# Where the weight sums of the seven-product form are made: eight sets in feed-forward steps 22 to 54, instead of four beside the weight decode and four in steps 22 to 36

## The chip, the cores and the metric

The kernel runs on one core of a Trainium2 chip. The metric is the device time of one execution in microseconds; lower is better. Engines are named as in the profile: PE (TensorE, the matrix unit), DVE (VectorE), ACT (ScalarE), POOL (GpSimd), SP (SyncE, which here only issues DMAs).

## The reference, cut to what matters

Eight batches of eight heads of sliding-window attention with a linear bias, then one feed-forward layer over the 4608 tokens, all in float32.

```python
scores = q @ k.T / sqrt(64)                 # q, k, v: (8, 8, 576, 64)
scores = where(0 <= rel < 128, scores - slope[h] * abs(rel), -1e9)
attn = softmax(scores) @ v
x = attn.transpose(0, 2, 1, 3).reshape(4608, 512)
h = x @ w_in                                # (512, 2048)
out = (h * sigmoid(1.702 * h)) @ w_out      # (2048, 512)
```

## The kernel before, in words

**Precision.** A float32 operand of the feed-forward layer is cut into a rounded high part and the rest (`res[:, 0]`, `res[:, 1]`; `xh`, `xl`; `gh`, `gl`), and a product of two operands is three matrix products: high by high, and the two mixed ones. ACT makes the high part with a cast, POOL makes the rest with a subtraction.

**Weights.** `w_in` and `w_out` are cut into 16 slices each, `w1[f]` and `w2[f]`, of 128x512 elements. They arrive as 64-bit words and are turned into split float32 by `decode`: an ACT operation into a tile `wc` (L226), two DVE operations by way of a PSUM tile `bits` (L228, L229), an ACT cast (L232) and a POOL subtraction (L233) into `w`. `bits` is taken from the PSUM ring `h_ps`, which has two buffers and also holds the up-projections. `wc` is taken from the SBUF ring with the tag `o`, which has five buffers (`OBUFS`) and also holds `wr`, `wh`, `xb`, `half` and `o`.

**Feed-forward, first form.** Tokens come in 18 chunks of 256. Chunks 0 to 11 are computed directly. One step is one slice `f` of one chunk: `up` (L579, 12 matrix products 128x256 into `h_ps`), the activation (ACT L584, DVE L585 into `g`, ACT L588 `gh`, POOL L589 `gl`), and `down` (L599, 6 products 128x512 into `acc0` and `acc1`). There are 192 such steps: chunk 0 with its first 8 slices (steps 0 to 7), chunk 1 (8 to 23), chunk 0's other 8 slices (24 to 31), then chunks 2 to 11. Between the two parts of chunk 0 its partial sums go to DRAM: ACT copies `acc` into `half` (L616), which frees `acc`, and SP writes it out (L618); at step 31 DVE adds it again (L623, L624).

**Decode.** Slices are decoded just ahead of the step that needs them, so decoding lasts until slice 15 of chunk 1, step 23.

**Attention.** One `tick` moves the attention units one stage further: loads (SP, L166), splits of q, k and v (ACT, and POOL L318, L329, L330), scores (PE L342 or L352), bias and minimum (DVE L369 or L380), exponents (ACT L392 or L399), normalisation (ACT L417 and POOL L420, or DVE L424), transposes (PE L438 or L461), and the product with v (PE L495 or L518). Batches 0 and 1 use one form, the lines named first; batches 2 to 7 use the second, heavier on DVE and POOL, and pass through `xb` (ACT L548) and DVE additions (L554, L557). Ticks are paced so that a chunk's tokens are there in time.

**Feed-forward, second form.** Chunks 12 to 17 are computed in pairs, with seven products instead of eight for each pair of weight slices (2j, 2j+1). This needs sums of weight blocks, S1 to S4, split again. `sums(j, a, b)` makes them: four DVE operations 128x256 in place (L653 to L656), then for each of the two tiles an ACT cast into `wh` (L659), a POOL subtraction (L660), and four DMAs of 128 KB (L663, L664) into DRAM tiles `part`. That is one set; there are eight, j = 0 to 7. `copy_out` writes the plain blocks (L641). The pairs read the parts from DRAM through a ring, after step 191.

**When the sums are made.** For j = 4 to 7 `decode_next` calls `sums` at once after it has decoded slice 2j+1, on the two tiles `wc` that the decode has just used: `kept` holds the first of them until the second is there. For j = 0 to 3 the `wc` tiles are long gone, so `rebuilt` adds the two parts of the split weight again (L646, DVE 128x512, into `wr`), two such additions a set, in steps 22, 25, 29 and 32:

```python
if made < F0 // 2 and now >= REBUILT[len(REBUILT) * made // (F0 // 2)]:
    sums(made, rebuilt(2 * made), rebuilt(2 * made + 1))
```

**What sets the order.** The program is written in this order, and a scheduler then places each instruction on its engine by its own estimate of times, under the data dependencies and the rings' buffers; each engine runs its own list strictly in order, and SP's list holds nearly all DMAs. So a change in one place moves instructions on all engines for a long way.

Of the kernel before, what the change touches and what calls it, by code (L numbers as in the profile page):

```python
# [24 lines left out]
NF = DFF // P  # L25
# [16 lines left out]
F0 = 8  # L42
# [5 lines left out]
COLS = 2 * P  # L48
RING = 5
LEAD = 6  # L50
REBUILT = range(22, 36)
COPIED = 64
COVER = 2
ORDER = "A11", "A12", "S2", "S3", "S1", "S4", "A22"
# [98 lines left out]
def tile_kernel(ctx: ExitStack, tc: tile.TileContext, q0, k0, v0, qT, kT, v, w_in, w_out, out):  # L153
# [51 lines left out]
    w1, w2 = [None] * NF, [None] * NF  # L205
# [7 lines left out]
        w1[f] = fetch(w_in[f], f"w1_{f}")  # L213
        w2[f] = fetch(w_out[f], f"w2_{f}")

    kept = {}

    def decode(st, name, pin=lambda ins: ins):

        words = st.bitcast(I32).rearrange("p (m two) -> p m two", two=2)  # L220
        top, low = words[..., 1], words[..., 0]
        c = ffn.tile([P, 512], I32, name="wc", tag="o", bufs=OBUFS)

        pin(nc.scalar.activation(c.bitcast(F32), top.bitcast(F32), AF.Prelu, scale=2.0 ** -112, alpha=2.0 ** 32))  # L226
        bits = ps.tile([P, 512], I32, name="bits", tag="h_ps", bufs=2)
        pin(nc.vector.tensor_scalar(bits, low, 29, None, ALU.logical_shift_right))  # L228
        pin(nc.vector.scalar_tensor_tensor(c, c, 3, bits, ALU.logical_shift_left, ALU.bitwise_or))  # L229
        w = c.bitcast(F32)  # L230
        res = const.tile([P, 2, 512], F32R, name=name, tag=name)
        pin(nc.scalar.copy(res[:, 0], w))  # L232
        pin(nc.gpsimd.tensor_tensor(res[:, 1], w, res[:, 0].bitcast(F32), ALU.subtract))  # L233
        if name.startswith("w1"):
            kept[name] = w
        return res


# [300 lines left out]
    def recall(ct):  # L539

        if ct in away:
            nc.sync.dma_start(home(ct), away.pop(ct))
# [90 lines left out]
    def part(j, name):  # L633

        at, side = divmod(j * len(ORDER) + ORDER.index(name), 2)
        return parts[at][:, side]
# [12 lines left out]
    def sums(j, a, b):  # L649


        a1, a2, b1, b2 = a[:, :COLS], a[:, COLS:], b[:, :COLS], b[:, COLS:]
        nc.vector.tensor_tensor(a1, a1, b1, ALU.subtract)  # L653
        nc.vector.tensor_tensor(b1, b1, b2, ALU.add)
        nc.vector.tensor_tensor(b2, b2, a1, ALU.subtract)
        nc.vector.tensor_tensor(a2, a2, b2, ALU.subtract)  # L656
        for t, names in ((b, ("S1", "S2")), (a, ("S3", "S4"))):
            hi = ffn.tile([P, 2 * COLS], F32R, name="wh", tag="o", bufs=OBUFS)
            nc.scalar.copy(hi, t)  # L659
            nc.gpsimd.tensor_tensor(t.bitcast(F32R), t, hi.bitcast(F32), ALU.subtract)  # L660
            for i, name in enumerate(names):
                cs = slice(i * COLS, (i + 1) * COLS)
                nc.sync.dma_start(part(j, name)[:, 0], hi[:, cs].bitcast(F32))  # L663
                nc.sync.dma_start(part(j, name)[:, 1], t[:, cs])  # L664
# [132 lines left out]
    units, due = [], []  # L797
# [18 lines left out]
    ticks, seen = 0, 0  # L816
# [31 lines left out]
    def fetch_upto(n):  # L848
        nonlocal fetched
        while fetched < min(n, NF):  # L850
            fetch_weights(fetched)
            fetched += 1
# [3 lines left out]
    def decode_next():  # L856
        nonlocal halves
        g, ws = halves // 2, (w1, w2)[halves % 2]

        pin = [tc.keep_in_program_order] if halves < PINNED else []  # L860
        ws[g] = decode(ws[g], f"w{1 + halves % 2}_{g}", *pin)
        halves += 1
        if ws is w1 and g >= F0 and g % 2:
            sums(g // 2, kept.pop(f"w1_{g - 1}"), kept.pop(f"w1_{g}"))

    tables()
    idle = ps.tile([P, DM], F32, name="acc0")
# [26 lines left out]
    now, credit = 0, 0.0  # L894
# [31 lines left out]
    made = 0  # L926
    flat = [(j, f) for j in jobs for f in range(j.f0, j.f1)]
    late = []
    for now, (j, f) in enumerate(flat):

        if halves < 2 * NF:
            owed += max(
                (2 * g + 2 - halves - owed) / max(need[g] - DECODE_AHEAD - now, 1)
                for g in range(halves // 2, NF))
            while owed >= 1 and halves < 2 * NF:
                owed -= 1
                fetch_upto(halves // 2 + 1 + FETCH_AHEAD)
                decode_next()

        advance(now)  # L940
        if made < F0 // 2 and now >= REBUILT[len(REBUILT) * made // (F0 // 2)]:
            sums(made, rebuilt(2 * made), rebuilt(2 * made + 1))
            made += 1
        if 0 <= now - COPIED < NF // 2 * 3:
            copy_out((now - COPIED) // 3, ("A11", "A12", "A22")[(now - COPIED) % 3])
        if j.begun and f == j.f1 - 2:
            j.refetch()
        if now == F0 + F0:
            recall(0)
        if now == len(flat) - 4:  # L950
            recall(S0 + 1)
        if now + 1 < len(flat):
            nj, nf = flat[now + 1]
            if nj is j:
                j.up(nf)
            else:
                begin(nj)
        if now < len(flat) - COVER:
            j.down(f)
            if f == j.f1 - 1:  # L960
                j.finish()
        else:
            late.append(f)

    assert made == F0 // 2 and ticks >= due[-1][0] + 3
    before = None
    for c in range(S0, NCH, 2):
        pair = Pair(c)
# [71 lines left out]
```

## Time and profile before

| | us |
|---|---|
| median of three executions (1045.43 to 1050.3) | 1047.8 |
| the profiled execution | 1047.39 |
| its span, first to last instruction | 1045.6 |
| PE busy in the span | 1027.1 |
| ACT / DVE / POOL busy | 675.8 / 651.1 / 621.2 |

The profiled execution lies 0.4 us below the median of the three. A busy PE is not PE at its peak: a matrix product's record lasts longer than the time after which the next may follow, so short holes between products are hidden in the busy time and have to be read from the starts. In the windows below, the columns are the stretch in us and its length, then each engine's busy time with the number of its instructions, the granted clock, the DMA share and GB/s. In a timeline a row gives start, duration, engine, line, operation, tiles, shape and count, and in brackets the engine's idle time before it and what ended it.

### The profile page before, as it was taken

To read this page: it belongs to the slowest core of one execution; us is meant where nothing else is said; L and a number is where in the kernel's file an instruction comes from. 1 tells how busy PE (TensorE), PEld (TensorE's weight loads), DVE (VectorE), ACT (ScalarE), POOL (GpSimd) and SP (SyncE) were. 2 spreads that over 40 slices of the span, in tenths; PEclk is the share of its full clock that TensorE was granted. 3 is DMA by queue.
4 is the path that set the end of the run, shared out by engine and by line. 5 is a ranking of instruction groups with operands and counts; after the bars stand their busy time and mean duration, and the time that the engine had idled before them with its cause. 6 is when DMAs were issued, how large, how long until landed. Compare 5 with 4: busy or idle time off the path is not lost.

```text
span 1045.6 us, 21874 instructions
## 1 busy us (share of the span) xinstructions
PE 1027.1 (98%) x6897; PEld 906.8 (87%) x6897; DVE 651.1 (62%) x2250; ACT 675.8 (65%) x1978; POOL 621.2 (59%) x858
## 2 busy tenths in 40 slices
PE   8899999999999999999999999999999999999998
PEld 5577778789999999999999999999898998998997
DVE  6786756367777677777777676766743445346343
ACT  6888855478787777877777786877633334335332
POOL 3687866568677677768667686766542224224221
PEclk9899999999999999999999999999999999999999
DMA  8995445423333233334323433432175556456551
GB/s 290 365 354 167 152 134 159 130 77 100 97 110 100 77 90 121 108 100 129 95 80 102 130 108 90 128 104 68 57 276 181 174 172 219 162 181 207 179 180 61
DMA packets 120275, 151.91 MB, mean 145 GB/s; under 512 B 40032, under 2 KB 96864, under 8 KB 120160
## 3 DMA queue, kind: packets, MB, share of 16 engines
q1 hardware_dynamic: 114400, 140.55, 43.2%
q10 hardware_dynamic: 5760, 9.96, 2.7%
q8 instruction: 55, 0.90, 0.4%
q14 instruction: 60, 0.49, 0.1%
HBM read 119.01 MB, written 31.46 MB: 144 GB/s over the span
## 4 chain that ended last, share of the span: by engine, by line
PE 89%; DMA 4%; DVE 3%; ACT 2%; issue 1%; POOL 1%; SPq 0%; POOLq 0%; ACTq 0%; DVEq 0%
PE h_ps L579 24%; PE acc L599 24%; PE accs L779 12%; PE X_ps L720 6%; PE s_ps L352 5%; PE x_ps L518 5%; PE Y_ps L720 4%; PE t_ps L461 4%; PE x_ps L495 2%; PE t_ps L438 1%; PE sb_ps L342 1%; DMA x<-xf 1%; PE s_ps L342 1%; DMA VV<-v 1%; DMA rk<-k 1%
## 5 line engine op out<-in xcount | busy, mean ns | idle before, releaser
L579 PE MATMUL h_ps<-xh,w 128*128 128x256 f32 x1536 | 245.7, 285 | 2.3 <-DVE g L585 1.4
L579 PEld LDWEIGHTS h_ps<-xh,w 128*128 128x128 f32 x1536 | 212.5, 189 | 18.5 <-DVE g L585 3.3
L599 PE MATMUL acc<-w,gh 128*128 128x512 f32 x768 | 216.3, 399 | 0.8 <-ACT half L616 0.4
L589 POOL TENSOR_TENSOR gl<-g,gh 128x256 fp32r<-128x256 f32 x192 | 144.7, 755 | 100.1 <-ACT gh L588 79.9
L732 POOL TENSOR_TENSOR gs<-g,gs 128x512 fp32r<-128x512 f32 x48 | 63.4, 1320 | 169.9 <-PE Y_ps L720 120.5
L599 PEld LDWEIGHTS acc<-w,gh 128*128 128x128 f32 x768 | 131.2, 188 | 21.3 <-ACT half L616 1.2
L779 PE MATMUL accs<-w,gs 128*128 128x512 f32 x576 | 148.3, 393 | 0.3 <-POOL gs L732 0.3
L579 PE MATMUL h_ps<-xl,w 128*128 128x256 f32 x768 | 138.2, 283 | 0.0
L330 POOL TENSOR_TENSOR K<-rk,K 128x384 fp32r<-128x384 f32 (+1 forms) x120 | 108.6, 905 | 43.0 <-ACT K L328 34.7
L599 PE MATMUL acc<-w,gl 128*128 128x512 f32 x384 | 125.7, 405 | 0.0
L585 DVE SCALAR_TENSOR_TENSOR g<-g,h_ps 128x256 f32<-128x256 f32 x192 | 80.0, 417 | 65.0 <-ACT g L584 62.9
L584 ACT ACTIVATE g<-h_ps 128x256 f32<-128x256 f32 x192 | 72.9, 381 | 70.4 <-PE h_ps L579 61.0
L779 PEld LDWEIGHTS accs<-w,gs 128*128 128x128 f32 x576 | 102.3, 189 | 17.6 <-POOL gs L732 0.7
L579 PEld LDWEIGHTS h_ps<-xl,w 128*128 128x128 f32 x768 | 112.0, 189 | 5.8 <-issue 1.5
L399 ACT ACTIVATE pb<-pb,mins 128x256 f32<-128x256 f32 (+2 forms) x216 | 104.7, 486 | 9.1 <-DVE mins L380 8.6
L588 ACT CAST gh<-g 128x256 fp32r<-128x256 f32 x192 | 77.6, 405 | 41.7 <-DVE g L585 33.4
L380 DVE CUSTOM_DVE_ANT_0 pb<-s_ps,bias 128x256 f32<-128x256 f32 (+3 forms) x240 | 86.1, 380 | 26.5 <-PE s_ps L352 23.4
L424 DVE TENSOR_SCALAR_CACHE_REDUCE pb<-pb,rec 128x256 f32<-128x256 f32 (+2 forms) x216 | 91.1, 454 | 2.9
L329 POOL TENSOR_TENSOR Q<-rq,Q 64x256 fp32r<-64x256 f32 (+1 forms) x120 | 81.8, 682 | 11.7 <-ACT Q L310 2.3
L480 DVE TENSOR_TENSOR pl<-t_ps,ph 128x512 fp32r<-128x512 f32 (+2 forms) x120 | 72.9, 607 | 16.7 <-ACT ph L474 15.6
L461 PE MATMUL t_ps<-ident,pb 128*128 128x128 f32 x408 | 76.7, 272 | 0.0
L352 PE MATMUL s_ps<-K,Q 128*128 128x256 f32 (+1 forms) x432 | 75.8, 288 | 0.0
(114 smaller groups left out, 2000.9 us busy)
## 6 DMA issues: line engine op xcount, KB each, us to landing
ring<-part SPq DMA_DIRECT2D x84, 512.0 KB, 3.3
rk<-kT SPq DMA_DIRECT2D x72, 192.0 KB, 2.8
rq<-qT SPq DMA_DIRECT2D x96, 128.0 KB, 2.6
out<-o ACTq DMA_DIRECT2D x34, 256.0 KB, 2.9
rw<-w_in SPq DMA_DIRECT2D x16, 512.0 KB, 6.7
rw<-w_out SPq DMA_DIRECT2D x16, 512.0 KB, 7.2
x<-xf SPq DMA_DIRECT2D x13, 512.0 KB, 3.5
xf<-x SPq DMA_DIRECT2D x13, 512.0 KB, 4.3
```

Of the source, the lines that this page charges most:

```text
L329: nc.gpsimd.tensor_tensor(Q[D:], rq[D:], Q[D:].bitcast(F32), ALU.subtract)
L330: nc.gpsimd.tensor_tensor(K2, rk, K1.bitcast(F32), ALU.subtract)
L352: nc.tensor.matmul(u.s[:b.rows, e, b.first:b.end], u.Q[:, b.q0 - u.q0:b.q0 - u.q0 + b.rows], k[:, ko:ko + b.end - b.first], start=(z == 0) ...
L380: nc.vector.tensor_tensor_reduce(b.p[ra:rb, cs:b.end], u.s[ra:rb, e, cs:b.end], bias[head][ra:rb, cs:b.end], -SCALE, BIG, ALU.add, ALU.min ...
L399: nc.scalar.activation(live, live, AF.Exp, bias=u.mins[:b.rows, e:e + 1], scale=-1.0, accum_out=u.sums[:b.rows, e, :1],)
L424: nc.vector.tensor_scalar(live, live, u.rec[:rows, e:e + 1], None, ALU.mult, ALU.add, u.rec[:rows, 2 + e:3 + e])
L461: nc.tensor.transpose(u.t[:c.n, w:w + b.rows], b.p[:b.rows, col:col + c.n], ident[:b.rows, :b.rows])
L579: nc.tensor.matmul(h, w1[f][:, z, k * P:(k + 1) * P], x[:, k], start=(n == 0), stop=(n == len(ops) - 1))
L589: nc.gpsimd.tensor_tensor(gl, g, gh.bitcast(F32), ALU.subtract)
L599: products.append(nc.tensor.matmul(acc, g[:, t * P:(t + 1) * P], w2[f][:, z], start=(f == self.f0 and n == 0), stop=(f == self.f1 - 1 and ...
L720: nc.tensor.matmul(bank, w[:, z, k * P:(k + 1) * P], x[:, y, k], start=start and i == 0, stop=i == len(ops) - 1, skip_group_check=True)
L779: products.append(nc.tensor.matmul(self.acc[t], g[:, y, t * P:(t + 1) * P], w2[f][:, z], start=(f == 0 and n == 0), stop=(f == NF - 1 and ...
```

## The change

All eight sets are made from the split weights by `rebuilt`, and `REBUILT` is longer, so that set j comes in step 22 + 4j: 22, 26, 30, ... 50. `decode` keeps nothing. For j = 4 to 7 two additions L646 a set are new; everything else of these four sets is moved, with its casts, subtractions and 32 DMAs.

```diff
-REBUILT = range(22, 36)
+REBUILT = range(22, 54)
...
-    kept = {}
...
-        if name.startswith("w1"):
-            kept[name] = w
         return res
...
         halves += 1
-        if ws is w1 and g >= F0 and g % 2:
-            sums(g // 2, kept.pop(f"w1_{g - 1}"), kept.pop(f"w1_{g}"))
...
-        if made < F0 // 2 and now >= REBUILT[len(REBUILT) * made // (F0 // 2)]:
+        if made < NF // 2 and now >= REBUILT[len(REBUILT) * made // (NF // 2)]:
             sums(made, rebuilt(2 * made), rebuilt(2 * made + 1))
             made += 1
...
-    assert made == F0 // 2 and ticks >= due[-1][0] + 3
+    assert made == NF // 2 and ticks >= due[-1][0] + 3
```

In the changed file a line stands 2 to 6 lines higher than before (L616 becomes L612, L646 becomes L642, L653 becomes L649). Each engine's list is the same up to the first set of the decode, near 78 us; from there on it differs in many small places up to about 740 us, and is the same again in the second form.

ACT's list at the end of chunk 0's first part, before. `half<-acc` are the two copies that free `acc`; `wh<-wc` are the casts of set 4.

```order
L417 ACTIVATE pb<-pb,rec 128x128
L417 ACTIVATE pb<-pb,rec 128x256
L588 CAST gh<-g 128x256
L659 CAST wh<-wc 128x512 x2
L616 COPY half<-acc_657 128x512
L584 ACTIVATE g<-h_ps 128x256
L588 CAST gh<-g 128x256
L616 COPY half<-acc_658 128x512
L226 ACTIVATE wc<-rw_9_619 128x512
```

The same place after the change.

```order
L413 ACTIVATE pb<-pb,rec 128x128
L413 ACTIVATE pb<-pb,rec 128x256
L584 CAST gh<-g 128x256
L388 ACTIVATE pb,totals<-pb,mins 128x128
L612 COPY half<-acc_657 128x512
L388 ACTIVATE pb,totals<-pb,mins 128x256
L612 COPY half<-acc_658 128x512
L224 ACTIVATE wc<-rw_9_619 128x512
```

The two casts of set 4 are gone from in front of the first copy; one exponent stands in front of each copy instead.

PE's list at the same place, before: the last products of chunk 0's first part into `acc_657` and `acc_658`, then chunk 1's slice 1 (`w_1`) and its first down-products into `acc_1261`, up to slice 2.

```order
L599 MATMUL acc_657<-w_7_973,gl 128x512
L599 MATMUL acc_658<-w_7_973,gl 128x512
L579 MATMUL h_ps<-xh,w_1_554 128x256 x8
L579 MATMUL h_ps<-xl,w_1_554 128x256 x4
L599 MATMUL acc_1261<-w_0_484,gh 128x512 x2
...
L599 MATMUL acc_1262<-w_1_594,gl 128x512
L579 MATMUL h_ps<-xh,w_2_606 128x256 x8
```

The same place after the change.

```order
L338 MATMUL sb_ps<-rk,rq 128x128
L338 MATMUL s_ps<-rk,rq 128x256
L338 MATMUL sb_ps<-rk,rq 128x256
L595 MATMUL acc_657<-w_7_973,gl 128x512
L595 MATMUL acc_658<-w_7_973,gl 128x512
L575 MATMUL h_ps<-xh,w_1_554 128x256 x8
L575 MATMUL h_ps<-xl,w_1_554 128x256 x4
L434 MATMUL t_ps<-ident,pb 128x128 x6
L595 MATMUL acc_1243<-w_0_484,gh 128x512 x2
...
L491 MATMUL x_ps<-pw,VV 64x128 x2
L575 MATMUL h_ps<-xh,w_2_606 128x256 x8
```

Attention of units that came later before (three score products, six transposes, a product with v) now stands between the feed-forward products.

DVE's list in batch 2's attention, before; `carry` and `xf` are the additions behind `xb`.

```order
L480 TENSOR_TENSOR pl<-t_ps,ph 128x512
L380 ISA pb,mins<-s_ps,bias_78 128x256
L380 ISA mins 128x1
L554 TENSOR_TENSOR carry<-x_ps,xb 64x128
L557 TENSOR_TENSOR xf<-x_ps,xb 64x128
L557 TENSOR_TENSOR xf<-x_ps,xb 64x256
L585 SCALAR_TENSOR_TENSOR g<-g,h_ps 128x256
L410 TENSOR_REDUCE rec<-totals 128x1
```

The same place after the change: set 5 (slices 10 and 11).

```order
L476 TENSOR_TENSOR pl<-t_ps,ph 128x512
L642 TENSOR_TENSOR wr<-w_10_1256 128x512
L642 TENSOR_TENSOR wr<-w_11_1366 128x512
L550 TENSOR_TENSOR carry<-x_ps,xb 64x128
L553 TENSOR_TENSOR xf<-x_ps,xb 64x128
L553 TENSOR_TENSOR xf<-x_ps,xb 64x256
L376 ISA pb,mins<-s_ps,bias_78 128x256
L376 ISA mins 128x1
L581 SCALAR_TENSOR_TENSOR g<-g,h_ps 128x256
L649 TENSOR_TENSOR wr<-wr 128x256
L406 TENSOR_REDUCE rec<-totals 128x1
L650 TENSOR_TENSOR wr<-wr 128x256
```

Two additions 128x512 stand ahead of the additions that free `x_ps`, and the set's other operations stand between the attention's and the activation's. Sets 6 and 7 stand further down in the same way; set 4's six operations stand around chunk 0's `half<-acc,half` at step 31, before batch 2's first DVE work. On SP's list the eight part writes of set 5 stand in one block between the loads `rv`, `rq`, `rk` of two later units, and so do those of sets 6 and 7.

## The prediction

> **What bounds the kernel now.** I read the page's busy line and the chain of work first, then windows of 26 us over the span, then the rows of the timeline where a window is poorer than its neighbours.
>
> ```profile
> PE 1027.1 (98%) x6897; PEld 906.8 (87%) x6897; DVE 651.1 (62%) x2250; ACT 675.8 (65%) x1978; POOL 621.2 (59%) x858
> PE 89%; DMA 4%; DVE 3%; ACT 2%; issue 1%; POOL 1%; SPq 0%; POOLq 0%; ACTq 0%; DVEq 0%
> ```
>
> PE is the bound: 98% busy, and 89% of the chain. The change leaves PE's work as it is, so it can gain only where PE has holes that the moved work makes, and lose only where the work makes new ones. The holes before 78 us lie ahead of the first set and stay.
>
> ```profile
> 78.00:104.00 26.00, 23.99 (x156) 18.36 (x154) 16.06 (x47) 21.00 (x60) 19.88 (x22) 1.00 0.52 169
> 104.00:130.00 26.00, 25.70 (x169) 20.95 (x170) 20.56 (x51) 21.63 (x60) 22.85 (x24) 1.00 0.49 156
> 130.00:156.00 26.00, 25.86 (x155) 19.37 (x153) 14.15 (x40) 15.24 (x47) 18.09 (x19) 1.00 0.46 137
> ```
>
> The columns are PE, PEld, DVE, ACT, POOL. In 78 to 104 us, where set 4 is made beside the decode, PE is idle for 2.0 us and its weight loads are lower than in the next window; the clock is 1.00. So the question is what PE waits for there.
>
> **The holes that the change can close.** First what products cost when nothing waits, from the chain of work (start, duration):
>
> ```profile
> 137.72 0.92 PE acc L599 x4
> 139.33 1.37 PE h_ps L579 x12
> ```
>
> So a 128x512 product takes 0.23 us, a 128x256 one 0.114. Now the timeline, PE's rows and then those of the engines that it waits for:
>
> ```profile
> 83.77 1.18 PE L599 MATMUL acc<-w,gh 128*128 128x512 f32 x4
> ...
> 85.47 0.63 PE L599 MATMUL acc<-w,gl 128*128 128x512 f32 x2
> 86.65 1.19 PE L579 MATMUL h_ps<-xh,w 128*128 128x256 f32 x8 [0.56 <-DVE g L585]
> 87.68 0.62 PE L579 MATMUL h_ps<-xl,w 128*128 128x256 f32 x4
> 88.74 0.74 PE L599 MATMUL acc<-w,gh 128*128 128x512 f32 x2 [0.45 <-ACT half L616]
> 89.32 0.39 PE L599 MATMUL acc<-w,gl 128*128 128x512 f32 x1
> 89.92 1.60 PE L599 MATMUL acc<-w,gh 128*128 128x512 f32 x4 [0.21 <-ACT gh L588]
> 90.79 0.30 PEld L599 LDWEIGHTS acc<-w,gh 128*128 128x128 f32 x2 [0.58 <-ACT half L616]
> 92.05 0.62 PE L599 MATMUL acc<-w,gl 128*128 128x512 f32 x2
> 93.32 1.20 PE L579 MATMUL h_ps<-xh,w 128*128 128x256 f32 x8 [0.65 <-DVE wc L229]
> ...
> 110.29 0.87 PE L495 MATMUL x_ps<-pw,VV 128*64 128x256 f32 x8 [0.24 <-DMA VV<-v]
> ```
>
> ```profile
> 87.06 1.15 ACT L659 CAST wh<-wc 128x512 fp32r<-128x512 f32 x2
> 88.11 0.58 ACT L616 COPY half<-acc 128x512 f32<-128x512 f32 x1
> 90.15 0.59 ACT L616 COPY half<-acc 128x512 f32<-128x512 f32 x1 [0.29 <-DMA part<-wh]
> 91.88 1.77 ACT L226 ACTIVATE wc<-rw 128x512 f32<-128x512 f32 x3 [1.14 <-DMA half<-half]
> 92.57 1.29 DVE L229 SCALAR_TENSOR_TENSOR wc<-wc,bits 128x512 int32<-128x512 int32 x2 [2.42 <-ACT wc L226]
> ```
>
> Hole by hole:
>
> 1. The two products at 85.47 are through at 85.93; the next starts at 86.65: 0.72, waiting for `g`, that is for a buffer of `h_ps`, while `bits` uses the other. The set's part in it is small, but the new order places three score products just ahead. I count 0.4 of it as closed.
> 2. The four products at 87.68 are through at 88.14; the next starts at 88.74: 0.60, waiting for the first copy `half`. The copy stood behind set 4's two casts (1.15 us). The new order has one exponent there and six transposes on PE: closed.
> 3. 89.32 plus 0.23 is 89.55; the next starts at 89.92: 0.37, for the cast `gh`, late behind the same copy: closed.
> 4. The four products at 89.92 take 1.60 against 1.18 at 83.77: 0.42, for the second copy, which itself waited for a buffer of the ring `o` that a part write of set 4 still held: closed, since no set holds buffers there any more.
> 5. 92.05 plus 0.46 is 92.51; the next starts at 93.32: 0.81, for `bits` and `wc` of slices 9 and 10, whose ACT operation waited 1.14 us for a buffer of `o` until `half` had been written out. With two `wc` and two `wh` fewer in the ring the buffer is there: closed.
> 6. At 110.29 PE waits 0.24 for v of a later unit. That load stands behind set 4's part writes on SP's list, and ahead of all sets in the new order: closed.
>
> That is 0.4 + 0.60 + 0.37 + 0.42 + 0.81 + 0.24 = 2.84 us; with the whole of the first hole 3.16. The lower end is 0: `bits` still shares `h_ps`, and PE could wait for the decode instead. I take 2.8, since four of the six holes have the sets' casts or buffers by name in their rows.
>
> **What the moved and added work costs.** One set made from the split weights is priced by the four made so before; the first row below is their own operations (DVE, ACT, POOL), the second the whole stretch.
>
> ```profile
> 136.00:185.00 49.00, 15.97 (x24) 4.92 (x8) 10.17 (x8) 1.00 0.50 153
> ...
> 136.00:185.00 49.00, 48.87 (x311) 37.92 (x310) 27.65 (x73) 27.93 (x85) 34.60 (x37) 1.00 0.50 153
> ```
>
> A set is 15.97/4 = 3.99 us on DVE, 1.23 on ACT, 2.54 on POOL. The added eight L646 are within it. With four sets in 49 us PE was idle for 0.13 us, so sets 0 to 3, whose steps hardly move, cost nothing again: DVE at 56% covers them. Set 4 now stands at chunk 0's second half, step 31; sets 5 to 7 belong to steps 42, 46 and 50.
>
> ```profile
> 187.77 1.29 DVE L623 TENSOR_TENSOR half<-acc,half 128x512 f32<-128x512 f32 x2
> 250.57 1.29 DVE L626 TENSOR_SCALAR o<-acc 128x512 f32<-128x512 f32 x2
> ```
>
> These are the ends of steps 31 and 47, so a step is (250.57 - 187.77)/16 = 3.9 us, and sets 5 to 7 fall near 231, 246 and 262 us. What is free there:
>
> ```profile
> 185.00:200.00 15.00, 15.00 (x100) 11.79 (x100) 4.60 (x13) 6.21 (x22) 5.95 (x8) 1.00 0.48 136
> ...
> 215.00:230.00 15.00, 15.00 (x109) 13.52 (x110) 10.94 (x45) 11.78 (x39) 9.36 (x14) 1.00 0.23 65
> 230.00:245.00 15.00, 15.00 (x108) 14.01 (x107) 11.48 (x50) 12.12 (x40) 11.60 (x21) 1.00 0.33 87
> 245.00:260.00 15.00, 15.00 (x109) 13.95 (x109) 11.90 (x50) 12.13 (x40) 13.02 (x21) 1.00 0.39 116
> 260.00:275.00 15.00, 15.00 (x111) 13.95 (x110) 11.63 (x47) 11.74 (x35) 10.33 (x17) 1.00 0.30 78
> ```
>
> Set 4 has 10.4 us of free DVE at 185 to 200: nothing. In 215 to 275 DVE works 45.95 of 60 us, POOL 44.31, ACT 47.77; three sets add 11.98, 7.63 and 3.69. DVE comes to 97%, POOL to 87%, ACT to 86%. It fits, by 2.1 us on DVE, if attention may shift by some microseconds. If each set must fit into its own 15 us, DVE is over by 0.47, 0.89 and 0.62, together 2.0 us. PE has no hole in these rows, so what DVE is late with, `g` or the additions that free `x_ps`, becomes a hole. I take 0.8, nearer to the fit, since ticks run ahead of the chunk that needs them; the ends are 0 and 2.0, and a rival below goes further.
>
> **SP and the ring.** The 32 part writes of sets 4 to 7 stand in blocks of eight between later units' loads, and SP stops at each until its cast or subtraction is done.
>
> ```profile
> SPq L663 <- ACT wh L659: 23.9, 5, 14.3
> ```
>
> Between 80 and 260 us SP stood still for such casts five times, once for 14.3 us, and the one hole of PE from a late load was the 0.24 us above. I take nothing, at most 3 x 0.24 = 0.7. Four of the five `o` buffers are taken by a set while `xb` needs one of them in batch 2; its price is in the 2.0 us. The eight `kept` references cost nothing themselves.
>
> **The sum.** -2.8 + 0.8 = -2.0 against the profiled execution, 1047.39: 1045.4. The median of the three runs is 0.4 higher, so I predict 1045.8.
>
> **A shared port.** DVE's sets and POOL do get in each other's way:
>
> ```profile
> 138.00 1.28 POOL L233 TENSOR_TENSOR w<-wc,w 128x512 fp32r<-128x512 f32 x1
> 138.07 1.76 DVE L646 TENSOR_TENSOR wr<-w 128x512 f32<-128x512 f32 x1 [0.61 <-DMA part<-wc]
> ...
> L646 DVE TENSOR_TENSOR wr<-w x8: 660/748/1784, 136.2 to 174.9; 128x512 f32<-128x512 f32 x8
> L653 DVE TENSOR_TENSOR wr<-wr x4: 407/516/843, 140.1 to 175.9; 128x256 f32<-128x256 f32 x4
> ...
> L589 POOL TENSOR_TENSOR gl<-g,gh 128x256 fp32r<-128x256 f32 x192 | 144.7, 755 | 100.1 <-ACT gh L588 79.9
> ```
>
> The addition that began 0.07 us into a POOL subtraction ended 0.55 us after that one's end, as if it had run only then; the shortest takes 0.66. The Trainium skill, in "SBUF — State Buffer", section "SBUF: two separate sides", says that VectorE and GpSimd share one pair of ports as an exclusive lock: a VectorE operation with two SBUF inputs and a GpSimd operation exclude each other for the whole instruction. By that rule, which these rows bear out, the sets run worst where POOL is busiest, and 245 to 260 us is such a place. At their shortest a set's six DVE operations take about 2 x 0.66 + 4 x 0.41 = 3.0 us; the measured 3.99 holds 1.0 of waiting, at a POOL share of 34.60/49 = 71%.
>
> **The rivals.**
>
> - *The late sets choke DVE.* If in 215 to 275 us each of a set's six operations waits out one whole POOL operation of 0.755 us, a set takes 3.0 + 4.5 = 7.5 us, three take 22.5, and DVE is over by 22.5 - 14.05 = 8.5 us, which PE waits out: 1047.8 - 2.8 + 8.5 = 1053.5. It ends slower than before as soon as a set costs PE more than 2.8/3 = 0.93 us. For it: POOL at 87%. Against: at 71% a set waited 1.0, not 4.5. I give it 0.12, for all outcomes above 1049.
> - *No gain.* The holes at 85 to 93 us belong to the change from chunk 0 to chunk 1, where `h_ps` is shared with `bits`; PE waits there for the decode in another place, or the new holes eat the old. 1047.8; 0.22.
> - *More gain.* The decode runs freely and attention runs ahead, so that the windows 78 to 104 and 130 to 156 come to the weight-load time of 104 to 130: (20.95 - 18.36) + (20.95 - 19.37) = 4.2 us of it, at 20.95 per 26 us 5.2 us: 1042.6. Against: the other window holds another mix of products. 0.14.
> - *The forecast*, holes closed and sets hidden, 1044 to 1047.3: 0.52.
>
> That the change doesn't do what it says holds for set 4 alone, which the scheduler makes seven steps ahead of step 38.
>
> **Range and chances.** The three runs before spread over -2.4 and +2.5 us around their median. The low end is 1042.0, the largest holes (-3.2) and a low median; the high end 1050.5, no gain and a high one. Outside lie parts of the first and third rival, under 0.2. About 0.5% is what a measurement can tell here: faster is below 1042.6, slower above 1053.0. Faster: half of the third rival and an edge of the forecast, 0.13. Slower: somewhat over half of the first, 0.07. Same: 0.80.
>
> **What would show it.** Right: between 78 and 104 us PE idle under 0.5 us and no wait for `half` or `wc`; the eight L646 of sets 4 to 7 between 185 and 275 us, and PE still without idle time there. Wrong: waits of PE for DVE `g` or for `x_ps` at 225 to 275 us with L646 or L653 running ahead of them, L646 over 1.2 us on the mean there, or holes as large as before at the first part's end of chunk 0.

## The result, and the profile after

| | before | after |
|---|---|---|
| median of the executions (us) | 1046.9 (7: 1045.2 to 1050.3) | 1054.05 (7: 1052.4 to 1058.2) |
| ratio to before, 95% interval | | 1.0073 [1.0060, 1.0086] |
| the profiled execution | 1047.39 | 1058.18 |
| its span | 1045.6 | 1056.4 |
| its mean granted clock of PE | 0.996 | 0.990 |

The change makes the kernel slower by 0.7%, some 7.5 us. A second measurement on the chip that ran the first experiments gave 1053.95 against 1046.49. The profiled execution of the changed kernel is the longest of its seven, so the sizes below are checked by taking causes away, not read from it alone. Line numbers of the changed kernel are 2 to 6 lower: the additions of a set are L642 and L649 to L652, the cast L655, the subtraction L656, the part writes L659 and L660, `g` is L581, `xl` L561.

The busy line of the page after, then its windows, in the columns of before:

```profile
PE 1033.1 (98%) x6897; PEld 911.8 (86%) x6897; DVE 660.1 (62%) x2258; ACT 674.5 (64%) x1978; POOL 623.2 (59%) x858
```

```profile
78.00:104.00 26.00, 24.50 (x173) 19.48 (x172) 15.39 (x52) 22.94 (x72) 17.32 (x21) 1.00 0.54 165
...
182.00:208.00 26.00, 23.29 (x140) 18.21 (x139) 11.20 (x40) 11.95 (x41) 14.50 (x17) 0.87 0.55 171
...
234.00:260.00 26.00, 22.35 (x144) 20.27 (x142) 22.07 (x73) 18.27 (x57) 22.92 (x31) 0.93 0.41 122
```

PE's share is still 98%, yet two windows stand out: 182 to 208, where set 4 begins, and 234 to 260, where set 6 is made. PE is idle for 2.7 and 3.7 us there, and the clock is 0.87 and 0.93. DVE is busy for only 43% and 85% of them. So DVE was not full; something on it came at the wrong time. In the first window, which was to gain, PE still lost 1.5 us.

**The first hole, step 31.** Rows picked from the timeline after, of ACT, POOL, SP, PE and DVE (start, duration; the bracket is the engine's idle time before the row and what ended it; here and below, rows of other operations in between are left out):

```profile
180.31 0.62 ACT L655 CAST wh<-wr 128x512 fp32r<-128x512 f32 x1 [2.19 <-DVE wr L651]
...
182.40 1.26 POOL L656 TENSOR_TENSOR wr<-wr,wh 128x512 fp32r<-128x512 f32 x1
...
184.64 0.42 SPq L166 DMA_DIRECT2D rk<-kT  x1
185.16 0.85 SPq L659 DMA_DIRECT2D part<-wh  x2
186.10 0.91 SPq L660 DMA_DIRECT2D part<-wr  x2
...
188.27 0.74 PE L595 MATMUL acc<-w,gl 128*128 128x512 f32 x2
...
188.96 1.26 POOL L656 TENSOR_TENSOR wr<-wr,wh 128x512 fp32r<-128x512 f32 x1 [1.26 <-DMA part<-wr]
189.12 1.65 DVE L642 TENSOR_TENSOR wr<-w 128x512 f32<-128x512 f32 x1 [3.16 <-DMA part<-wr]
190.69 0.41 DVE L581 SCALAR_TENSOR_TENSOR g<-g,h_ps 128x256 f32<-128x256 f32 x1
191.16 1.19 PE L575 MATMUL h_ps<-xh,w 128*128 128x256 f32 x8 [2.15 <-DVE g L581]
```

Read it backwards. PE waits for `g`. `g` stands behind set 4's first addition on DVE, and that addition stood idle for 3.16 us until a part write of set 3 gave back a buffer of the ring `o`. Set 3's cast was through at 180.93 and its subtraction at 183.66, but SP reached their writes at 185.16 and 186.10, since loads of later units stood ahead of them, and only when they had landed did the addition run. It then took 1.65 us, beside a POOL subtraction that lasted until 190.22; set 4's next addition of this shape took 0.67. So about 1.0 of the 2.3 us that PE lost is the addition's meeting with POOL, and the rest is the wait for the buffer.

**The second hole, set 6 beside the split of the next chunk's `xl`.** Rows of POOL, DVE and PE:

```profile
247.76 2.78 POOL L561 TENSOR_TENSOR xl<-xf,xh 128x256 fp32r<-128x256 f32 x4
248.06 4.13 DVE L650 TENSOR_TENSOR wr<-wr 128x256 f32<-128x256 f32 x1
249.44 0.28 PE L575 MATMUL h_ps<-xl,w 128*128 128x256 f32 x1
250.51 0.71 POOL L585 TENSOR_TENSOR gl<-g,gh 128x256 fp32r<-128x256 f32 x1
251.19 0.71 POOL L326 TENSOR_TENSOR K<-rk,K 128x256 fp32r<-128x256 f32 x1
251.98 0.79 POOL L325 TENSOR_TENSOR Q<-rq,Q 64x256 fp32r<-64x256 f32 x1
...
252.91 0.39 PE L514 MATMUL x_ps<-pl,VV 128*128 128x256 f32 x1 [3.19 <-DVE pl L476]
```

An addition of 128x256, which takes about 0.42 us alone, took 4.13: six POOL operations ran back to back beside it, from 247.76 to 251.90, and it ended 0.3 us after the sixth. `pl` and `g` stood behind it, and PE lost 3.4 us.

**The clock behind both.** Windows cut where the granted clock changes (PE, PEld, DVE, ACT, POOL, then the clock):

```profile
189.21:192.63 3.42, 1.48 (x12) 1.45 (x12) 3.42 (x9) 2.35 (x10) 3.10 (x4) 1.00 0.52 165
192.63:196.04 3.41, 3.41 (x21) 2.62 (x20) 3.34 (x9) 0.50 (x2) 0.41 (x1) 0.50 0.69 215
196.04:199.46 3.42, 3.42 (x13) 2.64 (x12) 0.74 (x2) 1.17 (x4) 0.26 (x1) 0.50 0.76 218
...
250.65:254.07 3.42, 1.16 (x7) 1.03 (x8) 3.42 (x9) 0.82 (x2) 2.05 (x3) 1.00 0.00 0
254.07:257.48 3.41, 3.41 (x15) 3.12 (x14) 3.20 (x17) 3.13 (x9) 2.91 (x3) 0.50 0.41 139
```

After a window in which PE was idle for about 2 us, PE ran at half speed for 6.8 us, and after the second hole for 3.4 us. PE is the bound, so this is lost time that no busy share shows.

**The place that was to gain.** SP and PE in the timeline after:

```profile
74.58 10.80 SPq L637 DMA_DIRECT2D part<-w  x5
...
90.23 1.30 SPq L614 DMA_DIRECT2D half<-half  x2
...
94.05 0.87 PE L491 MATMUL x_ps<-pw,VV 128*64 128x256 f32 x8 [1.50 <-DMA VV<-v]
```

The holes for `half` and `wc` at 86 to 93 us are gone, and PE now waits 1.5 us for a load of v. SP had stopped from 85.4 to 90.2 us for the write of `half`, with this load behind it.

### The profile page after: what moved, and what is told of

Read it like the earlier page. It is cut to its first block, busy times and chain, and to the rows that moved or that the text cites. A ratio compares the mean times of both kernels' runs of the same rounds, so it can differ in the third digit from the quotient of the medians.

```text
span 1056.4 us, 21869 instructions
## 1 busy us (share of the span) xinstructions
PE 1033.1 (98%) x6897; PEld 911.8 (86%) x6897; DVE 660.1 (62%) x2258; ACT 674.5 (64%) x1978; POOL 623.2 (59%) x858
## 4 chain that ended last, share of the span: by engine, by line
PE 90%; DMA 3%; DVE 2%; issue 1%; ACT 1%; POOL 1%; SPq 0%; POOLq 0%; ACTq 0%; DVEq 0%
PE h_ps L575 24%; PE acc L595 24%; PE accs L775 11%; PE X_ps L716 6%; PE s_ps L348 5%; PE x_ps L514 4%; PE Y_ps L716 4%; PE t_ps L457 4%; PE x_ps L491 2%; PE t_ps L434 1%; PE s_ps L338 1%; PE sb_ps L338 1%; DMA rk<-k 1%; DMA x<-xf 1%; PE acc L202 1%
## 5 line engine op out<-in xcount | busy, mean ns | idle before, releaser
L575 PE MATMUL h_ps<-xh,w 128*128 128x256 f32 x1536 | 249.4, 287 | 3.0 <-DVE g L581 2.9
L581 DVE SCALAR_TENSOR_TENSOR g<-g,h_ps 128x256 f32<-128x256 f32 x192 | 79.8, 416 | 56.5 <-ACT g L580 52.5
L457 PE MATMUL t_ps<-ident,pb 128*128 128x128 f32 x408 | 78.9, 273 | 0.0
```

What stands on the lines that cost most here:

```text
L457: nc.tensor.transpose(u.t[:c.n, w:w + b.rows], b.p[:b.rows, col:col + c.n], ident[:b.rows, :b.rows])
L575: nc.tensor.matmul(h, w1[f][:, z, k * P:(k + 1) * P], x[:, k], start=(n == 0), stop=(n == len(ops) - 1))
```

## The experiments

Times are medians; the kernel before ran beside each group of four kernels: 1046.49, 1046.7, 1046.76 and 1046.61. Differences between runs of two groups carry these 0.3 us as well. The letters in the expectations are theories: A, the two holes of the profile after; B, DVE's load by the late sets; C, the changed order of the program; R, the ring; P, the port; L, load; Q, SP's list; D, DVE and its port.

**1. The changed kernel again.** No edit.

> The changed kernel once more, for a second profile of it. Stall theory (A): the time lost sits in a few long holes of PE, each behind one late instruction on an engine's list, and in the half clock after them. Then the hole near 189 us (2.2 to 2.6 us, PE waiting for g on DVE, DVE's addition L642 waiting for a part write) comes again with some 7 us of clock 0.5 behind it, and the time is 1053 to 1055; the 4.1 us addition near 248 us belongs to chance and is there again or not. Load theory (B): DVE has too much work in 215 to 275 us; then many small holes lie there in both profiles, and the hole near 189 us is small change.

Measured: 1053.95, ratio 1.0069 [1.0055, 1.0083]. Both holes come again in the profile, of 2.1 us at 187 and 3.4 us at 248 us, the second with the same addition at 4.13 us beside the same six POOL operations, and the clock is halved behind them as before.

**2. Without the late sets.**

The edit is against the kernel before, cut:

```diff
-    kept = {}
...
-        if ws is w1 and g >= F0 and g % 2:
-            sums(g // 2, kept.pop(f"w1_{g - 1}"), kept.pop(f"w1_{g}"))
...
-            nc.sync.dma_start(r.bitcast(F32), parts[len(ring) % len(parts)])
+            nc.sync.dma_start(r.bitcast(F32), parts[len(ring) % (len(parts) // 2)])
```

> Sets 4 to 7 are not made at all (the pairs read the parts of sets 0 to 3 in their place), sets 0 to 3 stand in steps 22 to 32 as before. It leaves only the gain side of the change. Prediction's sum: holes of 2.8 us gone, so 2 to 3 us below the kernel before, 1044 to 1045. Theory A: no PE hole over 1 us behind 130 us, but the v load near 92 us may still be waited for (1.7 us in the changed kernel), so 0 to 2 us below before. If it is slower than before, the decode without the sets is itself the loss.

Measured: 1045.19, ratio 0.9986 [0.9978, 0.9995]. The same two windows in its trace:

```profile
182.00:208.00 26.00, 25.58 (x165) 20.16 (x165) 8.40 (x37) 12.10 (x43) 13.98 (x18) 1.00 0.46 136
234.00:260.00 26.00, 26.00 (x186) 24.11 (x186) 19.45 (x84) 19.66 (x63) 20.56 (x34) 1.00 0.37 103
```

So all that is lost lies in sets 4 to 7. (Sets 1 to 3 also go back by one or two steps here. Run 3 has them where the changed kernel has them, and PE is busy for 26.00 us of the first window there too.) Taking the late sets away from the decode gains 1.3 us at the most, not 2.8: PE waits for the load of v at 92 us here too, 1.6 us. And part of the 1.3 us has nothing to do with the decode. Where the first form ends and the second begins, PE waits once for `g` in the kernel before and not here, 0.8 us in these profiles (first the kernel before, then this one):

```profile
735.00:785.00 50.00, 49.12 (x325) 44.24 (x324) 27.83 (x78) 24.36 (x66) 24.22 (x33) 1.00 0.47 167
735.00:785.00 50.00, 49.94 (x333) 45.17 (x332) 27.41 (x77) 24.60 (x66) 23.90 (x33) 1.00 0.46 164
```

No set is made there; what differs is the order of the engines' lists.

**3. Set 4 out of step 31's way.**

```diff
-REBUILT = range(22, 54)
+REBUILT = 22, 26, 30, 34, 42, 44, 46, 50
```

> Only REBUILT differs from the changed kernel: set 4 in step 42 instead of 38, set 5 in 44, sets 0 to 3 and 6 and 7 in the same steps; the scheduler then puts no addition of set 4 ahead of step 31's end. Theory A: the hole near 189 us and its half clock (together 5 to 6 us) are gone, 1047 to 1049, unless a new long wait arises in batch 2. Theory B: all four late sets now lie in steps 42 to 54, so DVE is fuller there and the time is at least that of the changed kernel, 1054 or more.

Measured: 1058.33, ratio 1.0109 [1.0096, 1.0123]. The first hole is gone, but four sets now share batch 2. DVE and PE there:

```profile
248.69 1.59 DVE L642 TENSOR_TENSOR wr<-w 128x512 f32<-128x512 f32 x1
...
250.68 1.13 DVE L642 TENSOR_TENSOR wr<-w 128x512 f32<-128x512 f32 x1
...
252.27 0.73 PE L457 MATMUL t_ps<-ident,pb 128*128 128x128 f32 x3 [2.58 <-DVE pb L420]
```

Two additions ahead of the normalisation of `pb`, and PE loses 2.8 us. A wait removed at one place was paid at another: theory A alone is not enough, and the time is where B expected it. Not all of it is DVE's load in batch 2: at 735 to 785 us PE is idle for 2.7 us here, against 0.8 in the changed kernel.

**4. The late sets spread out, one to every 16 steps.**

```diff
-REBUILT = range(22, 54)
+REBUILT = 22, 25, 29, 32, 70, 86, 102, 118
```

> Sets 0 to 3 in steps 22, 25, 29, 32 as before, sets 4 to 7 in steps 70, 86, 102, 118: each in the middle of a chunk, 16 steps apart. Theory A: no ring wait at step 31 and no subtraction row of a chunk's start beside a set, so no long hole; 1045 to 1047.5. Theory B: 4 us of DVE in some 62 us is small, 1045 to 1048 too. A time of 1050 or more would speak for the shuffled order itself (theory C).

Measured: 1047.38, ratio 1.0006 [0.9997, 1.0015]. The same work costs 2.2 us over run 2, where the changed kernel costs 8.8: what is paid depends on where the sets stand. Theory C falls as the account of the 7.5 us, since the order changes here as widely.

**5. Without set 3's part writes.**

```diff
             for i, name in enumerate(names):
+                if j == 3:
+                    continue
...
```

> The changed kernel without the eight part writes of set 3 (its casts and subtractions stay; the second form reads other, written parts in place of set 3's). The place of every addition on DVE up to set 4 stays. Theory R (ring): the hole of PE at 187 to 189 us comes from set 4's first addition, which stands ahead of g on DVE and waits 3 us for a buffer of the ring o that a part write of set 3 holds, behind loads on SP. Without the writes the wait falls under 0.7 us, the hole under 0.5 us, and the half clock behind it (about 7 us) goes too: 1053.95 - 2.1 - 3.4 = 1048.4 (1047.3 to 1049.8). Theory L (load: it is DVE's work as such that makes g late): DVE has the same operations in the same places, so the hole stays at 1.5 us or more, 1053 to 1054.5. The hole at 247 us stays by both.

Measured: 1050.53, ratio 1.0038 [1.0026, 1.0050], 3.4 us less than the changed kernel. Set 4's two first additions, and another addition of a set further on:

```profile
184.82 0.69 DVE L642 TENSOR_TENSOR wr<-w 128x512 f32<-128x512 f32 x1
...
188.96 0.67 DVE L642 TENSOR_TENSOR wr<-w 128x512 f32<-128x512 f32 x1
...
242.73 3.06 DVE L651 TENSOR_TENSOR wr<-wr 128x256 f32<-128x256 f32 x1
243.41 1.41 POOL L561 TENSOR_TENSOR xl<-xf,xh 128x256 fp32r<-128x256 f32 x2
```

The wait for the buffer is gone, and with it the first hole and the half clock behind it, at the same places on DVE: the wait for the ring is its cause, and load is not. The addition, now earlier, takes 0.69 us; its meeting with POOL, 1.0 us of the hole, went with the wait. The second hole stays, 2.2 us here, with another of set 6's additions shut out for 3.06 us.

**6. Without the four 128x256 additions of set 6.**

```diff
-        nc.vector.tensor_tensor(a1, a1, b1, ALU.subtract)
+        if j != 6:
+            nc.vector.tensor_tensor(a1, a1, b1, ALU.subtract)
...
```

> The changed kernel without the four 128x256 additions of set 6 (its casts, subtractions and part writes stay, with other values). Theory P (port): the hole at 247 to 251 us comes from one of these additions, which takes 4.1 us instead of 0.4 because POOL runs six operations back to back beside it, with pl and g queued behind it on DVE. Without them the hole is under 0.6 us, and the half clock behind it (3.4 us at half speed) goes: 1053.95 - 3.4 - 1.7 = 1048.9 (1047.5 to 1050.0). Theory L (load): DVE is relieved of 4 x 0.42 = 1.7 us, so a hole of 1.5 us or more remains: 1051 to 1052.5. The hole at 187 us stays by both.

Measured: 1050.06, ratio 1.0046 [1.0029, 1.0064]; 3.9 us less than the changed kernel. The largest hole left at 234 to 260 us is 0.6 us. The value lies a little above the range of P and below that of L. Its ten executions differ by the clock: three with a mean clock of 0.990 or 0.991 took 1053.7 to 1055.7, the seven at 0.994 to 0.997 took 1048.2 to 1052.4. The first hole, 1.7 us in its profile, was not followed by a half clock there.

**7. Both edits.**

> Both of the other two edits. Theory R+P with the clock: both holes go, and the time comes to that of the kernel without the late sets, 1045.2, plus up to 1 us for what the late sets still cost: 1045.2 to 1046.6; the granted clock is 0.995 or more. If the two holes are two of several costs of crowding, 1048 to 1051 remains.

Measured: 1049.58, ratio 1.0026 [1.0018, 1.0035]. The first expectation missed, the second held: the two named holes are gone, and 4.4 us over run 2 remain. The two do not add up: 3.4 and 3.9 singly, 4.4 together. In these profiles 1.0 of the 4.4 us is PE's idle time at 735 to 785 us (1.08 us here, 0.06 in run 2), where leaving instructions out has moved the order again.

**8. Holes of growing length in the kernel before.**

```diff
-                nc.scalar.copy(self.p, self.X)
+                for _ in range(HOLES.get((self.c, j), 1)):
+                    nc.scalar.copy(self.p, self.X)
```

> The kernel before, with the copy p out of X in the second form repeated 8, 9, 10, ... 18 and 20 times at twelve places some 20 us apart (the result is the same). PE runs on through about 2.1 us of other products and then stands still, so the holes grow from about 0.9 us to 5.3 us in steps of 0.37. If the granted clock falls to 0.5 after an idle stretch of about 2 us already, as the two holes of the changed kernel suggest, then the 1 us windows behind the holes of 2 us and more (from about the 4th place on) show 0.5 for 3 to 7 us and those of 0.9 and 1.3 us none. If a hole must fill a whole window of 3.4 us, then only the longest ones (from 3.4 us, the 8th place on) show it, and 2 us holes never. Sum of the holes 36 us; with the half clock behind eight of them 1.7 to 3.4 us more each: a time of 1083 without and 1100 to 1112 with it.

Measured: 1120.49 in one execution. The holes came out longer than expected, 2.2 to 7.0 us, 53.7 us in all. PE's rows at the first and the third place, and the windows around them, cut in steps of 3.41 us on the grid on which the clock changes:

```profile
795.85 1.09 PE L722 MATMUL X_ps<-xT,ring 128*128 128x256 f32 x6 [2.02 <-ACT p L743]
...
845.33 0.98 PE L722 MATMUL X_ps<-xT,ring 128*128 128x256 f32 x6 [2.78 <-ACT p L743]
```

```profile
793.15:796.56 3.41, 1.39 (x9) 0.91 (x9) 0.53 (x2) 2.54 (x7) 1.27 (x1) 1.00 0.47 160
796.56:799.98 3.42, 3.42 (x13) 2.84 (x12) 0.43 (x1) 0.63 (x2) 0.00 (x0) 0.50 0.46 153
...
840.94:844.35 3.41, 1.60 (x8) 1.00 (x7) 0.18 (x1) 3.00 (x8) 1.28 (x1) 1.00 0.46 154
844.35:847.76 3.41, 2.43 (x14) 2.18 (x15) 0.85 (x2) 1.65 (x5) 0.00 (x0) 1.00 0.09 18
847.76:851.18 3.42, 3.42 (x25) 3.16 (x24) 0.42 (x1) 0.37 (x1) 0.00 (x0) 1.00 0.62 216
```

A hole of 2.0 us that lies within one step of the grid halves the clock for the next; one of 2.8 us that is cut in two by a step doesn't. Neither expectation had this: it is not the hole's length but PE's idle time within one step of 3.41 us. Over the profiles of all kernels here, of the steps at full clock behind 70 us those with clearly more than 2.2 us of idle time (worked out from the starts of PE's products, at the times that they take when nothing waits) were always followed by half clock and those with less than 2.0 never; between, both occur. The grid lies differently in each execution, so a hole of 2 us has its price in some executions only. Price: (1120.5 - 1046.7 - 53.7) us over 51.2 us at half clock, 0.39 us for each, from this one execution.

**9 to 12. The part writes off SP.** ACT issues the writes of `wh`, POOL those of the remainder, in the changed kernel (9), the kernel before (10), and that of run 4 (11, and 12 with the two writes of `half` on ACT too).

```diff
-                nc.sync.dma_start(part(j, name)[:, 0], hi[:, cs].bitcast(F32))
-                nc.sync.dma_start(part(j, name)[:, 1], t[:, cs])
+                nc.scalar.dma_start(part(j, name)[:, 0], hi[:, cs].bitcast(F32))
+                nc.gpsimd.dma_start(part(j, name)[:, 1], t[:, cs])
```

> The changed kernel with the 64 part writes taken off SP: ACT issues those of wh, which it has cast, and POOL those of the remainder, which it has subtracted. SP then stops for no set, and loads of q, k and v stand behind no part write; the scheduler draws sets 4 to 6 a few steps forward (behind g 35, 38 and 42 instead of 32 to 35, 42 and 46). Theory Q (the common cause of the holes is SP's list: part writes behind loads hold buffers of o, loads behind part writes hold up ACT and PE): the hole at 187 us goes, and so do the small ones by late loads at 270 to 280 us; set 6 no longer stands beside the four xl subtractions: 1046 to 1049, no hole over 1.2 us after 130 us, no half clock between 130 and 1000 us. Theory D (DVE and its port are too full in batch 2, whoever writes): holes of 1.5 us or more between 190 and 275 us remain, in new places: 1050 to 1055.

> The kernel before with the same edit of the queues. By Q the hole at 0.4 us for the buffer of o at 90 us and the late v load at 110 us go: 1045 to 1046.5. If the issues on ACT and POOL cost as much as they save: 1046.5 to 1048.

> Sets 4 to 7 at steps 70, 86, 102 and 118, one to every 62 us, as in the run with the four in mid-chunk, with the part writes on ACT and POOL. By Q the 2.2 us that the late sets cost there against the kernel without them shrink to 1 or less: 1045.2 to 1046.3. If it is DVE's work that costs, 1047 to 1048 as before this edit.

> The last one with the two writes half of chunk 0's first half on ACT too. SP stood still for them from 85.6 to 90.4 us with the load of v behind them for which PE waits 1.6 to 1.9 us at 92 us. With the load free at 85.6 us the hole at 92 us goes: 1.5 us less than the last one, 1043.5 to 1045, the fastest of all. If another load or the decode takes its place: no change against it.

Measured: 1064.65 [ratio 1.0143 to 1.0189], 1057.35 [1.0083, 1.0114], 1050.32 [1.0023, 1.0050] and 1049.78 [1.0018, 1.0040]. The first three missed their ranges, and theory Q falls with them: the queue edit costs 10.6 us in the kernel before and 2.9 in that of run 4. In run 12 the hole at 92 us is gone, but the time is that of run 11 within the intervals, as its second expectation had it. The group of POOL's issues in run 11, then DVE and PE in run 9:

```profile
L660 POOL DMA_DIRECT2D part<-wr x32 | 18.0, 564 | 0.3 <-POOL wr L656 0.3
```

```profile
217.28 2.51 DVE L642 TENSOR_TENSOR wr<-w 128x512 f32<-128x512 f32 x2
...
221.26 0.45 PE L514 MATMUL x_ps<-ph,VV 128*128 128x256 f32 x1 [3.27 <-DVE xf L553]
```

An issue occupies POOL for 0.56 us, 18 us in all. In run 9 the scheduler drew the late sets together: their first additions begin at 183, 199, 217 and 240 us, where the changed kernel has 189, 228, 244 and 272. They stand ahead of DVE's attention work, and the holes came back in new places, as D had it: three of 2.5 to 3.4 us, each with half clock. In run 10 PE is idle for 7.7 us between 78 and 182 us, against 2.4 before; whether the issues or the changed order do this was not taken apart. Of the places tried, SP was the cheapest for these writes.

**13 to 15. What remains after both holes.** The part writes of sets 3 to 7 left out (13), the sixteen 128x256 additions of sets 4 to 7 and set 3's writes left out (14), and both (15).

> The changed kernel without the part writes of sets 3 to 7 (the second form reads other, written parts); all additions, casts and subtractions stay. With the writes of set 3 alone left out it took 1050.5. Theory Q (SP, stopped by part writes, makes loads of q, k and v late in batch 2): now 1048 or less. Theory D (DVE's additions, each of them able to be shut out by POOL, are what costs): 1050 to 1051, as with set 3's writes alone left out, the hole near 245 us included.

> The changed kernel without set 3's part writes and without the sixteen 128x256 additions of sets 4 to 7; their eight 128x512 additions, casts, subtractions and part writes stay (other values). With set 6's four alone left out it took 1049.6. Theory D: sixteen additions less on DVE in batch 2 bring it to 1046 to 1047.5. Theory Q: 1049 to 1050, no change.

> Both: no part writes of sets 3 to 7 and no 128x256 additions of sets 4 to 7. If Q and D hold all of what is left: 1045.2 to 1046.2, the time without the late sets. If the casts (ACT), the subtractions (POOL) or the order cost as well: 1047 or more.

Measured: 1049.86 [1.0020, 1.0040], 1047.39 [0.9998, 1.0016] and 1046.10 [0.9985, 1.0002]. Leaving out the late sets' own writes gives 0.7 us beyond run 5, which the intervals don't separate; leaving out their additions gives 2.2 beyond run 7. The time is D's, but only a part of it is saved in batch 2. PE's idle time in us (the stretch less PE's busy time), from one profile each:

| | 182 to 286 us | 735 to 785 us |
|---|---|---|
| kernel before | 0.00 | 0.88 |
| changed kernel | 6.36 | 0.77 |
| run 2 | 0.42 | 0.06 |
| run 3 | 4.12 | 2.66 |
| run 7 | 1.02 | 1.08 |
| run 14 | 0.27 | 0.12 |
| run 15 | 0.00 | 0.81 |

From run 7 to run 14 batch 2's stretch gives 0.75 us and the other, where no set is made, 0.96. So in these profiles DVE's additions in batch 2 cost less than 1 us beyond the two holes, and the order at the end of the first form makes as much; that the order is the cause there is read from the traces and not tested by a run. The last 0.9 us from run 15 to run 2 do not lie in batch 2 either: PE has no idle time there, and 0.75 us more than run 2 at 735 to 785.

**16. The load of v let through.** Run 4's kernel with all part writes on SP, and the two writes of `half` on ACT.

```diff
-                    nc.sync.dma_start(self.sums[-1], o)
+                    nc.scalar.dma_start(self.sums[-1], o)
```

> Sets 4 to 7 at steps 70, 86, 102 and 118 with all part writes on SP, as in the run that took 1047.4, and only the two writes half on ACT. SP then doesn't stand still from 85.6 to 90.4 us with v's load behind; the hole of 1.7 us at 92 us goes: 1045.5 to 1046.2, faster than the kernel before by 0.3 to 1.0. If another wait takes its place: 1047 to 1047.6.

Measured: 1045.46, ratio 0.9985 [0.9976, 0.9994]. SP and PE around 90 us, in run 4 and then here:

```profile
88.74 1.30 SPq L614 DMA_DIRECT2D half<-half  x2
90.09 0.42 SPq L166 DMA_DIRECT2D VV<-v  x1
...
92.59 0.87 PE L491 MATMUL x_ps<-pw,VV 128*64 128x256 f32 x8 [1.55 <-DMA VV<-v]
```

```profile
87.84 0.37 SPq L166 DMA_DIRECT2D VV<-v  x1
...
91.39 0.87 PE L491 MATMUL x_ps<-pw,VV 128*64 128x256 f32 x8
```

The wait is gone, and this kernel, with the late sets spread out, beats both: 1.1 us below the kernel before, 8.5 below the changed one.

## Why the prediction was wrong, step by step

Predicted were 1045.8 us and a range up to 1050.5; measured were 1054.05. One rival, at a chance of 0.12, had the direction. In the sum three terms at or near nothing were wrong, the gain was at most half of what was counted, and one term was missing.

- **"Set 4 has 10.4 us of free DVE at 185 to 200: nothing."** This is the step that failed first. Free time of an engine is not a place in its list. The addition stood ahead of `g`, waited 3.2 us for a buffer, and DVE's free time passed while it stood there. Price with its half clock: 3.4 us (run 5).
- **"I take nothing, at most 3 x 0.24 = 0.7", for SP and the ring.** The same hole from the other side. The prediction looked at loads behind part writes and bounded those by 0.24 us each. It did not ask who waits for a part write itself: the next set, by way of the ring `o`. Yet SP's list as a whole is not the bottleneck (runs 9 to 13).
- **"I take 0.8, nearer to the fit", for sets 5 to 7.** Without the first hole the late sets still cost 5.3 us over run 2 (1050.53 against 1045.19). The sum of busy times was not far off: sets 5 to 7 took 15.2 us of DVE where 11.98 were counted, most of the excess in one addition, and DVE stands at 85% in the window that lost most. But PE's loss comes from single additions that stand ahead of `pl`, `pb` and `g`, one of them for 4.1 us, which an average does not price. Set 6's four cost 3.9 us (run 6). What is left when both holes are closed is in part such additions and in part the changed order at 735 to 785 us (runs 7 and 14).
- **The shared port.** The mechanism was named, its price was taken from the mean: 1.0 us a set, or one POOL operation of 0.755 us for each addition. The trace after has an addition that waits out six in a row. The Trainium skill, "SBUF — State Buffer", section "SBUF: two separate sides", says that whichever operation starts first holds the pair for its whole length; it doesn't say who is next, and here a waiting DVE operation was passed over by POOL five times. As the page has it, the lock takes in DVE operations with two SBUF inputs; in the trace of before, `pl` has one input in PSUM and ran in 0.69 us beside the same four subtractions:

```profile
243.51 2.83 POOL L565 TENSOR_TENSOR xl<-xf,xh 128x256 fp32r<-128x256 f32 x4
...
244.73 0.69 DVE L480 TENSOR_TENSOR pl<-t_ps,ph 128x512 fp32r<-128x512 f32 x1
```

- **The sign set to show it.** The prediction would have taken L646 over 1.2 us on the mean as proof of choking. The eight of the late sets have 1.01; the harm shows in one group alone, L650, through one of its four. A mean was the wrong instrument. The other sign, PE waiting for `x_ps` behind such an addition, did come, at 252.91. Rows of the trace after, grouped over 185 to 285 us:

```profile
L642 DVE TENSOR_TENSOR wr<-w 128x512 f32<-128x512 f32 x8 | 7.9, 1012 | 3.2 <-DMA part<-wr 3.2
...
L650 DVE TENSOR_TENSOR wr<-wr 128x256 f32<-128x256 f32 x4 | 5.5, 1377 | 0.1
```

- **"I take 2.8", for six holes closed.** The holes named did close. But at 92 us the load of v was late, so run 2 lies 1.3 us below the kernel before, not 2.8, and in the two profiles 0.8 us of the difference is a wait at 735 to 785 us that the six holes have nothing to do with. For each hole the prediction asked what ended it and not what would be late next, though it had the writes of `half` on SP before it. Run 16 shows the rest of the gain where that load is let through: 1.9 us.
- **The clock was left out.** Over 13 executions of the changed kernel the mean clock is 0.9931, over the 44 of the kernel before that ran beside runs 1 to 8 it is 0.9963. That is 6.7 us more at half clock; at 0.39 us each, the price from run 8, I estimate 2.6 us of the 7.5. The price of a hole of PE is not its length, once it is 2 us.
- **The rival "late sets choke DVE"** gave 1053.5 and came near, by another sum: of the 7.5 us that were lost the clock makes about 2.6, and of the first hole's 2.3 us more than half is a wait for the ring and no choking.

Open are two things: why the half clock lasted two steps behind the first hole and one behind the second; and the overlap of the two holes' prices (run 7), of which the runs show only that the holes shift and shrink when one is taken away, and that PE's idle time at 735 to 785 us differs from kernel to kernel.

## What to carry to other kernels

Price a moved operation by its place in its engine's list: what it waits for there, and what stands behind it; free time on that engine covers nothing while the operation at its head waits. Follow a ring of buffers to whoever gives them back, a DMA's place in SP's list included, and ask of each closed hole what is late next. Spread optional work thinly: the same four sets cost 8.8 us between steps 31 and 54 and 2.2 us at one to every 16 steps. And look at the whole span after each edit: a scheduler that orders anew changed PE's idle time by up to 2.6 us at a place some 500 us behind the sets.

## What the runs showed of the hardware

- **The clock.** Half clock comes in steps of 3.41 us on a fixed grid, as the Trainium skill, "TensorE: Matmul & The Clock Gate", section "Part 1: The HAM clock gate (the "warmup" mystery)", has it; there the clock falls after an idle window of about 3.4 us. Here PE need not be idle for the whole of it: clearly more than 2.2 us of idle time within one step were enough every time, and a hole of 2.8 us across two steps did nothing (run 8). One microsecond at half clock cost 0.39 us in run 8's one execution.
- **The port.** A DVE addition with two SBUF inputs was kept waiting by six POOL operations in a row, 4.13 us instead of 0.42, in two executions alike (the changed kernel and run 1).
- **POOL as issuer.** A DMA of 128 KB issued from POOL occupied it for 0.56 us (run 11).
